# Softmax denominators of most blocks: from TensorE matmuls to a DMA transpose and GpSimd sums

## The chip, the cores and the metric

The kernel runs on one core of a Trainium2 chip, in one launch. The metric is the device time in microseconds of that core, lower is better. A profile is one execution recorded by the hardware profiler; its span runs from the first to the last instruction of the program.

## What is computed

Four batches of 12,544 tokens with 128 channels go through an induced attention block and then through a max-out feed-forward layer:

```
x: (4, 12544, 128)   inducing: (32, 128)   w1, w2: (128, 1024)   w_out: (1024, 128)
mab(q, kv):  a = softmax(q kv^T / sqrt(128));  return a @ kv
h   = mab(inducing, x)          # per batch: 32 rows
y   = mab(x, h)                 # per batch: 12544 rows, softmax over the 32 rows of h
out = max(y @ w1, y @ w2) @ w_out
```

The second softmax has 32 terms for each token. Its denominator is one number for each token: the sum of 32 exponentials. The kernel keeps the exponentials unnormalised through the whole feed-forward layer and divides each output row by its denominator at the very end.

## The kernel before

**Tiling.** A batch is 98 chunks of 128 tokens. Chunks are taken in blocks of at most sixteen: a block has four quarters, and a quarter has up to four chunks. There are 28 blocks. For each block `stage` writes one tile `e2` of 128 partitions by 512: partition 32 q + m holds the exponential of inducing row m for the tokens of quarter q, and column 128 t + j is token j of the quarter's chunk t. Block 0 and blocks later than it go through these steps:

- `phase` (matmuls on L990): small matmuls with 32 rows of weights, four quarters side by side, give (w2 - w1) applied to y for all 1024 hidden columns; ScalarE (L1006) or VectorE (L1009) turns each PSUM bank of 512 columns into a `relu` tile. In the same rows a matmul with `m1` (also L990) starts the output bank with the linear part.
- `final_one` (L809): 8 matmuls of 128 x 128 for each chunk add the relu part to the output bank; 3,136 in all. This is most of TensorE's work.
- `evict_group` (L836): VectorE multiplies the output bank of a group (mostly 4 chunks) by `rp`, the reciprocal of the denominators, into an `o` tile (5 buffers), and SyncE stores it (L861).
- `dens` is called by `final_one` when the first group of a block is about to start and the block has no `rp` yet. It serves the block, and the next one too if that is staged. For each chunk column t it runs one full matmul on L641 with 128 columns of `e2` as weights against `ones_q`, 128 x 4, and one VectorE reciprocal (L651) then writes `rp`.

**Next batch.** While batch b is worked on, batch b+1 is prepared: GpSimd issues seven loads (`load_x`, L165), SyncE issues 14 DMA transposes of `x` into `xT` (`transpose_x_dma`, L171), TensorE takes the scores (`pool_scores`, L308), SyncE transposes their exponentials `eu` into `eT` (`pool_turn`, L345) in six pieces, and TensorE sums with them (`pool_accum`, L364), two pieces v = u-1, u for each call.

**Order.** All five engines have a hand order (`manual_schedule`). The program is written out by a loop that keeps a small clock of its own (`ck`) for TensorE, ScalarE and VectorE and chooses the next piece from it; side jobs stand in a list `pending` and are issued when `ready` says so; a table `DEV` changes the choice at some steps. So the order is fixed when the program is built, and each engine and each DMA queue works through its own list in that order. SyncE's list holds the stores, the transposes of `x` and the transposes of `eu`; an entry that waits holds all behind it.

Of the kernel before, what the change touches and what calls it, by code (L numbers as in the profile page):

```python
# [9 lines left out]
F16 = mybir.dt.float16  # L10
F32 = mybir.dt.float32
AF = mybir.ActivationFunctionType
ALU = mybir.AluOpType
# [3 lines left out]
INF = 1e9  # L17
# [85 lines left out]
def kernel(  # L103
# [9 lines left out]
    nc = tc.nc  # L113
    B, N, C = x.shape
    M = inducing.shape[0]
# [10 lines left out]
    consts = ctx.enter_context(tc.tile_pool(name="consts", bufs=1))  # L126
    big = ctx.enter_context(tc.tile_pool(name="big", bufs=1))
    etp = ctx.enter_context(tc.tile_pool(name="etp", bufs=3))
    e2p = ctx.enter_context(tc.tile_pool(name="e2p", bufs=NE2))
    smp = ctx.enter_context(tc.tile_pool(name="smp", bufs=2))  # L130
    relup = ctx.enter_context(tc.tile_pool(name="relup", bufs=2))
    outp = ctx.enter_context(tc.tile_pool(name="outp", bufs=5))
# [41 lines left out]
        st[b]["T", j] = ck.pe  # L174

    identity16 = consts.tile([128, 128], F16, name="identity16")
    identity32 = consts.tile([128, 128], F32, name="identity32")
    ones32 = consts.tile([128, 128], F32, name="ones32")
    ones16 = consts.tile([128, 128], F16, name="ones16")
    warm = consts.tile([128, 512], F16, name="warm")  # L180
    ones_q = consts.tile([128, 4], F16, name="ones_q")

    ind_sb = consts.tile([M, C], F32, name="ind_sb")
    w2h = relup.tile([128, 4096], F16, name="w2h", tag="relu0")[:, 0:J]
    w1h = relup.tile([128, 4096], F16, name="w1h", tag="relu1")[:, 0:J]
    w21 = consts.tile([C, J], F16, name="w21")
# [2 lines left out]
    w1out = consts.tile([C, C], F16, name="w1out")  # L189
    inducingT = consts.tile([C, M], F16, name="inducingT")  # L190
    m1bd = consts.tile([128, 4, C], F16, name="m1bd")
    rep32 = consts.tile([128, 128], F32, name="rep32")
    repd = consts.tile([128, 128], F32, name="repd")
    diag = consts.tile([128, M], F32, name="diag")
    pace = consts.tile([128, 1], F32, name="pace")

    with tc.manual_schedule(engines={ET.PE, ET.DVE, ET.Activation, ET.Pool, ET.SP}):
# [14 lines left out]
        nc.gpsimd.dma_start(out=woutp, in_=moe_w_out.rearrange("(jb j) c -> j jb c", j=128))  # L212
        nc.vector.memset(warm, 0.0)
        nc.vector.memset(ones16, 1.0)
        nc.vector.memset(ones32, 1.0)
        nc.vector.memset(ones_q, 0.0)
        for q in range(4):
            nc.vector.memset(ones_q[32 * q : 32 * (q + 1), q : q + 1], 1.0)
# [129 lines left out]
        def pool_accum(b, u):  # L348

            bi, ps = bank([128, 512])  # L350
            ck.wait(ck.bank[bi], "p1")
            last = u == NU - 1
            if u == 1:
                st[b]["hacc"] = smp.tile([128, C + 1], F32, name=f"hacc_{b}", tag="hacc")
            acc = st[b]["hacc"]
            if last:
                nc.vector.reduce_sum(out=acc[:, C : C + 1], in_=st[b]["es"], axis=AX.X)
                ck.on_dve(st[b]["eu", u][1], 0.1)
            for v in (u - 1, u):
                eT = st[b]["eT", v][0]  # L360
                st[b]["sum", v] = True
                for j in range(4):
                    for g in range(4):
                        nc.tensor.matmul(  # L364
                            out=ps[32 * g : 32 * (g + 1), 0:128],
                            lhsT=eT[:, j, 32 * g : 32 * (g + 1)],
                            rhs=xn_of(b, U * v + 4 * g + j),
                            start=(j == 0 and v < u),
                            stop=(j == 3 and v == u and not (last and g < REST)),
                            tile_position=(0, 32 * g),  # L370
                            skip_group_check=True,
                        )
            if last:
                et = st[b]["et"][0]
                for g in range(4):
                    pairs = [(warm[:, 0:M], ones16[:, 0:1], 128, 1)]
                    if g < REST:
                        pairs = [
                            (et[:, g, :], xn_of(b, U * NU + g), 0, 128),
                            (et[:, g, :], ones16[:, 0:1], 128, 1),  # L380
                        ]
                    for lhsT, rhs, lo, n in pairs:
                        nc.tensor.matmul(
                            out=ps[32 * g : 32 * (g + 1), lo : lo + n],
                            lhsT=lhsT,
                            rhs=rhs,
                            start=False,
                            stop=True,
                            tile_position=(0, 32 * g),
                            skip_group_check=True,  # L390
                        )
            end = ck.run(0.58 if last else 0.49, "col")
            n = C + 1 if last else C
            if u == 1:
                nc.vector.tensor_copy(out=acc[:, 0:n], in_=ps[:, 0:n])
            else:
                nc.vector.tensor_add(out=acc[:, 0:n], in0=ps[:, 0:n], in1=acc[:, 0:n])  # L397
            ck.bank[bi] = ck.on_dve(end, 0.22)
            if last:
                st[b]["esrr"] = ck.bank[bi]  # L400
            if last and b + 1 < B:
                for i in range(7):
                    load_x(b + 1, i, acc[:, C : C + 1] if i == 0 else None)

# [115 lines left out]
        def weights_1b():  # L520
            for h in range(2):
                nc.gpsimd.tensor_sub(w21[:, 512 * h : 512 * (h + 1)], w_of[h][0], w_of[h][1])
# [44 lines left out]
        for b in range(B):  # L567
# [6 lines left out]
                blocks.append(Block(quarters, (0,) if not blocks else (0, 1, 2, 3) if shape == (4, 3, 2, 1) else ()))  # L574
            assert c0 == K

        def stage(blk):
            bi, ps = bank([128, 512])
            wd = blk.width
            some = [qu for qu in blk.quarters if qu]  # L580
            ck.wait(max(ck.bank[bi], st[some[0].b]["hT4r"]), "stage bank")
            for q in range(4):
                qu = blk.quarters[q] or some[0]
                hq = st[qu.b]["hT4"][:, 32 * q : 32 * (q + 1)]
                xT = xT_tiles[qu.b % 2]
                lo = qu.c0 if qu.c0 + wd <= K else K - wd
                pieces = [(0, qu.c0, min(wd, K - qu.c0))]
                if pieces[0][2] < wd:
                    pieces.append((pieces[0][2], lo, wd - pieces[0][2]))
                for t, c, n in pieces:  # L590
                    nc.tensor.matmul(  # L591
                        out=ps[32 * q : 32 * (q + 1), 128 * t : 128 * (t + n)],
                        lhsT=hq,
                        rhs=xT[:, c : c + n, :],
                        start=True,
                        stop=True,
                        tile_position=(0, 32 * q),
                        skip_group_check=True,
                    )
            end = ck.run(0.054 * wd, "col")  # L600
            uid[0] += 1
            blk.e2 = e2p.tile([128, 512], F16, name=f"e2_{uid[0]}", tag="e2")
            nc.scalar.activation(  # L603
                out=blk.e2[:, 0 : 128 * wd], in_=ps[:, 0 : 128 * wd], func=AF.Exp,
                scale=st[0]["rs"] if blk.b == 0 else scale,
            )
            blk.staged = ck.bank[bi] = ck.on_act(end, 0.05 + wd * 128 / 1200.0)
            blk.staged = max([blk.staged] + [st[qu.b].get("hwdr", 0.0) for qu in some])
        relu_of = {}

        def relu_slot(blk, q):
# [110 lines left out]
        groups = [g for _, _, g in sorted(groups, key=lambda e: e[:2])]  # L722
        for n, g in enumerate(groups):
            g.blk.last_group[g.q] = n
        state = {"g": 0, "mm": 0, "lin": 0, "done": 0, "issued": 0}
        ptr = [[0, 0] for _ in range(4)]
        chunks_done = [0]

# [203 lines left out]
        def phase(jobs):  # L932
            free = sorted(range(8), key=lambda j: ck.bank[j])
            got = []
            for j in jobs:
                while j[0] == "L" and "m1" not in st[j[2].blk.b]:
                    f, a = pending.pop(0)
                    f(*a)
            for (kind, q, a, u), bi in zip(jobs, free):
                _, ps = bank([128, 512], only=bi)  # L940
# [73 lines left out]
                state["issued"] += 1  # L1014

        jobs_at, due = {}, {}
        DONE0 = [0, 98, 196, 294]

        def at(n, f, *a):
            jobs_at.setdefault(n, []).append((f, a))  # L1020
            if f in (pool_scores, pool_accum):
                due[f, a] = n
# [21 lines left out]
                at(base + int(t_first + t_step * j), transpose_x_dma, b, j)  # L1044

        pending = []

        def ready(f, a):

            d = st[a[0]]  # L1050
            now = ck.pe
            if f is pool_scores and a[1] >= NEU and ("eT", a[1] - NEU) not in d:
                return False
            if f is pool_turn and a[1] >= NEU and ("sum", a[1] - NEU) not in d:
# [72 lines left out]
        phase(plan_phase(False))  # L1127
        pending.append((small_m1, (0,)))
        state["stage"] = 2
        weights_1b()  # L1130
        START = ck.pe
        step = -1
        while state["g"] < len(groups) or held:
# [24 lines left out]
            if tp < INF and lag() <= 128 + LIMIT and now:  # L1158
                if how != 3 and column_work(len(jobs) + 1, how == 4):
                    continue  # L1160
                phase(jobs)
            elif tf < INF:
                keep_busy(tf)
                ck.wait(tf, "relu")
                final_one()
            elif tp < INF:
                phase(jobs)
            elif pending:
                f, a = pending.pop(0)
                f(*a)  # L1170
            else:
                raise AssertionError(("stuck", state, ptr, chunks_done, jobs, pending[:3]))
        assert not pending and not jobs_at

# [28 lines left out]
```

## Time and profile before

| | |
|---|---|
| median of 3 runs | 327.38 us (327.37 to 327.85) |
| profiled execution, span | 325.6 us |
| outside the span: median less span | 1.7 us |
| TensorE busy | 319.8 us, 98% of the span |
| VectorE busy | 283.1 us, 87% |
| ScalarE busy | 281.7 us, 87% |
| GpSimd busy | 25.6 us, 8% |
| denominators: matmuls on L641, reciprocals on L651 | 102 and 15 |
| DMA | 53.65 MB, mean 165 GB/s |

The profile page has no time of its own for the profiled execution besides the span; what lies around the span is taken as the difference to the median of the runs. PE is TensorE, DVE VectorE, ACT ScalarE, POOL GpSimd, SP SyncE; PEld are the weight loads of TensorE, which overlap its matmuls, and SPq is SyncE's queue. Matmuls are pipelined, so a matmul's duration is longer than the distance from its start to the start of the next one; what a matmul costs the stream is that distance.

### The profile page before, as it was taken

The numbers are of one execution on the slowest core, as the hardware profiler recorded it, in microseconds if no ns is written. First come the engines' busy times: TensorE is split into PE (matmuls) and PEld (weight loads), VectorE is DVE, ScalarE is ACT, GpSimd is POOL, SyncE is SP. The second block draws the span as 40 slices with busy tenths as digits, with TensorE's granted clock in tenths as the row PEclk, the third lists the DMA queues.
The fourth block names the chain that finished last, engine by engine and source line by source line (L and its number), as shares of the span: only waits on it lengthen the run. The fifth ranks groups of instructions, "written<-read, shape, count | busy, mean of one in ns | idle before, by whom it ended". The sixth has DMA issues, their size and how long they took to land.

```text
span 325.6 us, 12570 instructions
## 1 busy us (share of the span) xinstructions
PE 319.8 (98%) x5404; PEld 243.0 (75%) x5404; DVE 283.1 (87%) x509; ACT 281.7 (87%) x560; POOL 25.6 (8%) x51
## 2 busy tenths in 40 slices
PE   7999999999999999999999999999999999999996
PEld 3876777777767777777777777777777777778785
DVE  3359989989989998998989999998989999999973
ACT  3679899999989899998888999989969999999961
POOL 7452030000040000000040000000000000000000
PEclk9999999999999999999999999999999999999999
DMA  8999999976279999993389999992312312222233
GB/s 204 208 206 214 286 246 212 172 207 134 97 150 245 225 248 209 201 203 86 116 162 243 214 234 232 190 192 86 115 66 101 113 68 98 90 108 99 85 115 112
DMA packets 70823, 53.65 MB, mean 165 GB/s; under 512 B 52176, under 2 KB 55408, under 8 KB 70768
## 3 DMA queue, kind: packets, MB, share of 16 engines
q1 hardware_dynamic: 64656, 38.63, 49.2%
q0 software_dynamic: 6112, 14.22, 22.3%
q8 instruction: 42, 0.69, 0.9%
q14 instruction: 13, 0.11, 0.1%
HBM read 28.33 MB, written 25.69 MB: 166 GB/s over the span
## 4 chain that ended last, share of the span: by engine, by line
PE 95%; DVE 1%; DMA 1%; ACT 0%; issue 0%; ACTq 0%; DVEq 0%
PE ps L809 61%; PE ps L990 22%; PE ps L591 2%; PE ps L232 2%; PE ps L308 2%; PE ps L364 1%; DMA xf<-in_x_dram 1%; PE ps L248 1%; DVE relu L1009 1%; PE ps L280 1%; PE ps L641 1%; PE ps L766 1%; PE ps L271 1%; PE ps L657 0%; PE ps L473 0%; PE ps L409 0%
## 5 line engine op out<-in xcount | busy, mean ns | idle before, releaser
L1006 ACT ACTIVATE relu<-ps 128x512 f16<-128x512 f32 x461 | 244.8, 602 | 26.6 <-PE ps L990 18.1
L1009 DVE TENSOR_SCALAR relu<-ps 128x512 f16<-128x512 f32 x323 | 206.8, 682 | 16.9 <-PE ps L990 15.3
L809 PE MATMUL ps<-woutp,relu 128*128 128x128 f16 x3136 | 217.3, 220 | 0.0
L809 PEld LDWEIGHTS <-relu 128*128 128x128 f16 x3136 | 176.7, 98 | 39.6 <-issue 29.1
L990 PE MATMUL ps<-e,hwd 32*128 32x512 f16 (+2 forms) x880 | 88.7, 360 | 0.0
L836 DVE TENSOR_TENSOR o<-ps,rp 128x512 f32<-128x512 f32 (+3 forms) x108 | 68.5, 634 | 5.5 <-PE ps L809 3.4
L990 PEld LDWEIGHTS <-hwd 32*128 32x128 f16 x880 | 24.9, 91 | 21.1 <-issue 1.0
L990 PE MATMUL ps<-m,e 32*128 32x128 f16 x381 | 38.8, 217 | 0.0
L990 PEld LDWEIGHTS <-e 32*128 32x128 f16 x381 | 21.3, 93 | 2.6
L165 POOL DMA_DIRECT2D xn<-in_x_dram x31 | 17.0, 557 | 8.2 <-DMA xn<-in_x_dram 4.3
L236 DVE COPY xT<-ps 128x512 f16<-128x512 f16 (+3 forms) x11 | 5.5, 504 | 7.8 <-PE ps L232 7.7
L319 ACT ACTIVATE eu<-ps 128x512 f16<-128x512 f32 x18 | 10.8, 615 | 0.0
L603 ACT ACTIVATE e<-ps 128x512 f16<-128x512 f32 (+2 forms) x21 | 10.5, 577 | 0.0
L164 POOL COPY pace<-hacc 128x1 f32<-128x1 f32 x2 | 0.4, 184 | 114.8 <-DVE hacc L397 114.8
L591 PE MATMUL ps<-xT,hT 128*32 128x512 f16 (+3 forms) x114 | 8.9, 362 | 0.0
L239 ACT COPY xT<-ps 128x768 f16<-128x768 f16 (+3 forms) x11 | 6.1, 556 | 2.7 <-PE ps L232 2.6
L232 PE MATMUL ps<-identity,xn 128*128 128x128 f16 x98 | 7.4, 219 | 0.4 <-DVE xn L661 0.3
L232 PEld LDWEIGHTS <-xn 128*128 128x128 f16 x98 | 5.6, 97 | 1.6 <-DVE xn L661 1.1
L257 ACT ACTIVATE et<-ps 128x448 f16<-128x448 f32 (+4 forms) x11 | 4.5, 413 | 2.6 <-PE ps L248 2.6
L308 PE MATMUL ps<-xT,inducingT 128*32 128x512 f16 x72 | 6.5, 385 | 0.0
L591 PEld LDWEIGHTS <-hT 128*32 128x32 f16 x114 | 3.3, 94 | 4.1 <-issue 3.0
L364 PE MATMUL ps<-xn,eT 128*32 128x128 f16 x288 | 5.5, 220 | 0.0
(96 smaller groups left out, 108.2 us busy)
## 6 DMA issues: line engine op xcount, KB each, us to landing
out_dram<-o SPq DMA_DIRECT2D x90, 256.0 KB, 2.4
xn<-in_x_dram POOLq DMA_DIRECT2D x24, 448.0 KB, 11.8
out_dram<-o SPq DMA_DIRECT2D x10, 128.0 KB, 3.0
xn<-in_moe_w_dram POOLq DMA_DIRECT2D x4, 256.0 KB, 14.1
xn<-in_x_dram POOLq DMA_DIRECT2D x4, 224.0 KB, 10.2
xT<-xn SPq DMA_TRANSPOSE x42, 4.3
xf<-in_x_dram SPq DMA_DIRECT2D x1, 512.0 KB, 3.9
xf<-in_x_dram SPq DMA_DIRECT2D x1, 384.0 KB, 4.3
```

The lines of the kernel that those rows point to most:

```text
L165: nc.gpsimd.dma_start(out=xn_at[b, i][:, 0:n, :], in_=xr[b, :, k0 : k0 + n, :])
L232: nc.tensor.transpose(ps[:, j, :], xn[:, g + j, :], identity16)
L308: nc.tensor.matmul(out=ps[32 * g : 32 * (g + 1), :], lhsT=inducingT, rhs=xT_tiles[b % 2][:, U * u + 4 * g : U * u + 4 * (g + 1), :], start ...
L319: nc.scalar.activation(out=eu, in_=ps, func=AF.Exp, scale=scale, accum_out=st[b]["es"][:, u : u + 1])
L364: nc.tensor.matmul(out=ps[32 * g : 32 * (g + 1), 0:128], lhsT=eT[:, j, 32 * g : 32 * (g + 1)], rhs=xn_of(b, U * v + 4 * g + j), start=(j = ...
L591: nc.tensor.matmul(out=ps[32 * q : 32 * (q + 1), 128 * t : 128 * (t + n)], lhsT=hq, rhs=xT[:, c : c + n, :], start=True, stop=True, tile_p ...
L603: nc.scalar.activation(out=blk.e2[:, 0 : 128 * wd], in_=ps[:, 0 : 128 * wd], func=AF.Exp, scale=st[0]["rs"] if blk.b == 0 else scale,)
L809: nc.tensor.matmul(out=g.ps[:, 128 * c : 128 * (c + 1)], lhsT=g.blk.relu[q][:, 128 * (jb * w4 + t) : 128 * (jb * w4 + t + 1)], rhs=woutp[: ...
L836: nc.vector.tensor_mul(osb[:, 0:n, :], g.ps[:, 0 : n * C].rearrange("p (s c) -> p s c", s=n), rp)
L990: nc.tensor.matmul(**seq[i])
L1006: nc.scalar.activation(out=dst, in_=src, func=AF.Relu)
L1009: nc.vector.tensor_scalar(out=dst, in0=src, scalar1=0.0, scalar2=None, op0=ALU.max)
```

## The change

For 20 of the 28 blocks the denominators no longer come from TensorE. When such a block is staged, a job `turn_e2` is put in `pending`. It issues on SyncE a DMA transpose of the `e2` tile into `ed` (token on the partition, then chunk, quarter and the 32 terms), and on GpSimd five additions that halve the 32 terms step by step (16, 8, 4, 2, 1) and one `pow` with exponent -1; the result `rd` takes the place of `rp`. `dens` is unchanged and serves the blocks that have no `rp` when their first group starts.

`ready` lets a `turn_e2` go only if at least 20 chunks of earlier blocks are still to be finished, the block is staged, the last turn was at least 9 us before and the last loads of the next batch at least 22 us before (all on the builder's clock); turns start after 18 chunks. The subtraction of the weights on GpSimd (`weights_1b`) is issued at that point too, in the same place of GpSimd's list. To make room in SBUF, the constants that are needed at the start alone (`identity32`, `rep32`, `ind_sb`, `diag`) share the first buffer of `relu3`, `ones16` shrinks and `ones32` goes.

The core of the diff:

```diff
+    edp = ctx.enter_context(tc.tile_pool(name="edp", bufs=2))
...
-    identity32 = consts.tile([128, 128], F32, name="identity32")
-    ones32 = consts.tile([128, 128], F32, name="ones32")
-    ones16 = consts.tile([128, 128], F16, name="ones16")
+    head = relup.tile([128, 4096], F16, name="head", tag="relu3").bitcast(F32)
+    identity32 = head[:, 0:128]
+    rep32 = head[:, 128:256]
+    ind_sb = head[0:M, 256:384]
+    diag = head[:, 384:416]
+    ones16 = consts.tile([128, 2], F16, name="ones16")
...
+    minus1 = consts.tile([128, 16], F32, name="minus1")
...
             if last and b + 1 < B:
+                state["loads"] = ck.pe
                 for i in range(7):
                     load_x(b + 1, i, acc[:, C : C + 1] if i == 0 else None)
...
+            if state.get("turns"):
+                pending.append((turn_e2, (blk,)))
+
+        def turn_e2(blk):
+
+            if blk.rp is not None:
+                return
+            state["turned"] = ck.pe
+            wd = blk.width
+            uid[0] += 1
+            ed = edp.tile([128, 4, 128], F16, name=f"ed_{uid[0]}", tag="ed")
+            nc.sync.dma_start_transpose(
+                ed[:, 0:wd, :], blk.e2[:, 0 : 128 * wd].rearrange("p (j t) -> p j t", j=wd)
+            )
+            den = edp.tile([128, 16], F32, name=f"den_{uid[0]}", tag="den")
+            half = edp.tile([128, 16, 16], F32, name=f"half_{uid[0]}", tag="half", bufs=1)
+            cur = ed[:, 0:wd, :].rearrange("p j (q m) -> p (j q) m", q=4)
+            n = M // 2
+            while n >= 1:
+                dst = half[:, 0 : 4 * wd, 0:n] if n > 1 else den[:, 0 : 4 * wd, None]
+                nc.gpsimd.tensor_tensor(out=dst, in0=cur[:, :, 0:n], in1=cur[:, :, n : 2 * n], op=ALU.add)
+                cur = half[:, 0 : 4 * wd, :]
+                n //= 2
+            rp = edp.tile([128, 4, 4], F32, name=f"rd_{uid[0]}", tag="rd", bufs=7)
+            nc.gpsimd.tensor_tensor(
+                out=rp[:, 0:wd, :].rearrange("p t q -> p (t q)"),
+                in0=den[:, 0 : 4 * wd],
+                in1=minus1[:, 0 : 4 * wd],
+                op=ALU.pow,
+            )
+            blk.rp = rp[:, 0:wd, :]
+            blk.turned = ck.pe
...
+        def turns_on():
+            weights_1b()
+            state["turns"] = True
...
+        at(18, turns_on)
...
+            if f is turn_e2:
+                blk = a[0]
+                if blk.rp is not None:
+                    return True
+                ahead = sum(len(g.chunks) for g in groups[state["g"] :] if g.blk.index < blk.index)
+                return ahead >= 20 and blk.staged <= now and state["turned"] + 9.0 <= now and state["loads"] + 22.0 <= now
...
-        weights_1b()
```

## The prediction

> **What bounds the kernel now.** I read the page's busy shares and its chain first.
>
> ```profile
> PE 319.8 (98%) x5404; PEld 243.0 (75%) x5404; DVE 283.1 (87%) x509; ACT 281.7 (87%) x560; POOL 25.6 (8%) x51
> ```
>
> ```profile
> PE 95%; DVE 1%; DMA 1%; ACT 0%; issue 0%; ACTq 0%; DVEq 0%
> ```
>
> TensorE is busy for nearly all of the span and is 95% of the chain that ended last. A busy PE need not be a full PE, so the waits come next.
>
> ```profile
> ACT relu L1006 <- PE ps L990: 18.1, 45, 1.9
> DVE relu L1009 <- PE ps L990: 15.3, 35, 1.5
> ...
> PEld L809 <- DVE relu L1009: 0.3, 1, 0.3
> ```
>
> ScalarE and VectorE wait for TensorE (18.1 and 15.3 us); TensorE waits for a relu once, 0.3 us. TensorE's own stream is the bound, so what it no longer issues is gained in full, and any wait put in its way is lost in full. Then one place where denominators are made, from the timeline (start, length, instructions), and the two lines as such:
>
> ```profile
> 104.72 0.45 PE L809 MATMUL ps<-woutp,relu 128*128 128x128 f16 x5
> 105.01 0.34 PE L641 MATMUL ps<-ones_q,e 128*128 128x4 f16 x8
> 105.21 0.78 PE L809 MATMUL ps<-woutp,relu 128*128 128x128 f16 x11
> ```
>
> ```profile
> L641 PE MATMUL ps<-ones_q,e x102: 163/165/168, 25.9 to 316.7; 128*128 128x4 f16 x102
> ```
>
> Eight matmuls hold the stream from 105.01 to 105.21: 25 ns each, not the 165 ns that one lasts, since they overlap.
>
> **TensorE: what goes.** The order in which the changed kernel's instructions stand has 32 matmuls for denominators, at 5 places, instead of 102 at 15. The runs of matmuls between switches of kind (222 of the L990 kind, 26 of scores and sums) are as many as before. So 70 x 25 ns = 1.8 us goes, all on the path.
>
> A rule of the Trainium skill would make it more: "TensorE: Matmul & The Clock Gate", section "LDWEIGHTS (loading the stationary operand)", takes a weight load of 128 columns as 128/1.2 = 107 ns, so that 70 would be an estimated 7.5 us; here the load lies under other work, and the 25 ns of the timeline decide.
>
> **VectorE.** Ten reciprocals go: six of 348 ns, two of 297, two of 274, together 3.2 us. VectorE waits 15.3 us for TensorE as it is, so this brings nothing. One relu moves from VectorE to ScalarE (0.60 us against 0.68), hidden by the 18.1 us that ScalarE waits.
>
> **SyncE: what comes.** Twenty transposes, sixteen of them 4 x 128 columns like those of `eu` on L345:
>
> ```profile
> 64.01 2.57 SPq L861 DMA_DIRECT2D out_dram<-o  x3
> 66.67 2.64 SPq L345 DMA_TRANSPOSE eT<-eu  x2
> 69.41 0.53 SPq L861 DMA_DIRECT2D out_dram<-o  x1
> 70.03 2.54 SPq L345 DMA_TRANSPOSE eT<-eu  x2
> 72.66 2.10 SPq L861 DMA_DIRECT2D out_dram<-o  x2
> ```
>
> Two take 2.63 us until the next issue (70.03 to 72.66), 1.3 us each. The queue goes from one issue to the next without a pause from 50 to 76 us, so a transpose put in there moves all behind it by 1.3 us. The guard keeps turns off the loads, where stores have least room (at 93 to 106 and 165 to 176 us a store lands 0.7 to 2.5 us before its `o` buffer is needed; at the turns it is 5 us and more), but not off the transposes of `x` and `eu`. In the built order one turn stands behind the eighth transpose of `x` (52.8 us), one behind the fourteenth (64.0), one behind the second of `eu` (69.4), one behind the fifth. So the third and fourth of `eu` come 3 x 1.3 = 3.9 us later. The view of L345 in 71.2 to 72.6 us has these two, and TensorE's timeline their reader:
>
> ```profile
> DMA to landing us min/median/max: 2.4/3.2/4.0
> ```
>
> ```profile
> 77.15 1.08 PE L364 MATMUL ps<-xn,eT 128*32 128x128 f16 x64
> ```
>
> The fourth is issued at 71.3 and lands 4.0 us later, 75.3; the last 16 of the 64 matmuls read it, at 77.8. In the changed kernel they come at 77.6 (8 matmuls fewer before) and the issue at 75.2. With a landing of 2.4 us there is no wait (77.6), with 4.0 it is 1.6 us, with the middle of the two, 3.2, it is 0.8 us. I take 0.8: the same piece behind the same neighbours took 4.0, its twin 2.4.
>
> The next narrowest places: the scores at 61.1 read a transpose issued at 54.8 that landed at 59.5; 1.3 us later is 60.8, against 60.9: nothing, 0.5 us if it is unlucky. The sums at 138.4 read an `eu` transpose that landed at 135.1, behind two turns: 137.7, against 138.4 less 0.6 plus the 0.8 lost before: nothing. The others have over 1.5 us left by the same count.
>
> **GpSimd and the wait on it.** The first eviction of a turned block (L836) now waits for `rd`; behind it in VectorE's list stand the relus of the following phases, and TensorE waits for those. Chain: issue, landing (2.3 to 4.2 us for `eu`, median 2.8), five additions and a power. The nearest rows:
>
> ```profile
> L522 POOL TENSOR_TENSOR w<-xn,xn 128x512 f16<-128x512 f32 x2 | 2.5, 1270 | 10.3 <-DMA xn<-in_moe_w_dram 10.3
> L164 POOL COPY pace<-hacc 128x1 f32<-128x1 f32 x2 | 0.4, 184 | 114.8 <-DVE hacc L397 114.8
> ```
>
> Six instructions are at least 6 x 0.18 = 1.1 us and, if each cost as much as 512 columns, 7.6 us. The additions have 256 columns down to 16: estimated 0.65, 0.4, 0.3, 0.2, 0.2; no row has a power on GpSimd, I take 0.6 for it: 2.4 us, nearer the copy's end since five of six are short. With 2.8 the chain is 5.2 us. Room: the first turn from 52.8 to the eviction at 63.9, 11.1 us; the second from 65.3 to 75.6, 10.3; the fifth 119.0 to 131.7, 12.7; the others 14.8 (the fourth, 80.2 to 95.0) and more. Covered; even 7.6 + 2.8 is 10.4.
>
> A rule speaks against it: "GPSIMD Engine Reference", section "Instruction dispatch", puts the first call of a freshly loaded kernel at about 6 us of code loading; that would make the first chain an estimated 11.2 us and cost 0.1 us once. L522's first subtraction (1.27 us, the second 1.27) shows nothing of the kind, and no row here has the power.
>
> **At nothing.** `weights_1b` keeps its place in GpSimd's list (41 us), and its reader, L473, starts at 92.7. The start constants in `relu3` are last read at 22.2 us (L449), before the first relus; were they read later, the first relu of that buffer would wait. The memsets of the start change size only.
>
> **Sum.** Against the profiled execution: 325.6 - 1.8 + 0.8 = 324.6 us of span; with the 1.7 us around it, 326.3. The span and these 1.7 us make the median of the runs, 327.4, so the sum holds for it as well.
>
> **Rivals.**
> *A turn costs the queue more than its issue* (slower). If the next transpose only gets going when the turn has landed (2.3 us at least), the pushes are 6.9 instead of 3.9 us at the same sums, and the wait there grows from 0.8 to 3.8 us: 327.4 - 1.8 + 3.8 = 329.4. It turns the result slower from a wait of 2.5 us, that is a push of 1.9 us a turn. For it: the 16 DMA engines are busy for 0.96 of the stretch from 46 to 82 us, and one transpose held the queue 5.67 us at 107.1. Against it: transposes issued 1.3 us apart each landed in 2.3 to 4.2.
> *GpSimd's chain is longer than its room.* A power that takes 6 us more makes the chain 11.2 us: 0.1 us at the first, 0.9 at the second turn, 327.3. At 14 us of chain it would be 2.9 + 3.7 + 1.3 = 7.9 us. For it: no row; against it: five of the six are plain additions and all but three turns have over 14 us.
> *The matmuls filled time in which TensorE would wait anyway*: 327.4. The waits (0.3 us for a relu) speak against it.
>
> **Chances.** The forecast has 0.72: 0.60 with a wait up to 1.1 us, 0.12 with more, up to 1.6 (no change). Slow turns 0.13 (0.10 slower, 0.03 no change), GpSimd 0.08 (0.04 and 0.04), no gain 0.07. A measurement of this kernel tells about 0.2%, 0.65 us: faster is below 326.73, slower above 328.03. Faster 0.60, same 0.26, slower 0.14. The range goes from 325.3 (no wait anywhere, 325.6, and 0.3 us of the small gaps that ten reciprocals fewer may close) to 328.2, with 0.12 left out above and some 0.05 below.
>
> **What would show it.** L641 x32, L651 x5 and about 1.0 us of the stream at the first; a wait of TensorE for a DMA (`eT`) near 78 us, at most 1.6 us; L836 never waiting for GpSimd; six GpSimd instructions in 2 to 3 us. Wrong it would be if evictions wait for `rd`, if stores hold VectorE by their `o` buffer, or if L364 or L308 wait for longer than 2.5 us.

## The result, and the profile after

The changed kernel takes 329.05 us, the median of 22 runs (327.44 to 332.16); the kernel before took 327.58 us in the runs beside it. The ratio is 1.0044, with an interval of 1.0024 to 1.0065: slower, where the forecast was faster. The profiled execution has a span of 327.5 us against 325.6.

The engines' busy times and the chain that ended last, from the changed kernel's page:

```profile
PE 319.5 (98%) x5334; PEld 241.4 (74%) x5334; DVE 280.1 (86%) x498; ACT 281.8 (86%) x561; POOL 113.2 (35%) x171
```

```profile
PE 91%; DMA 4%; DVE 3%; ACT 1%; issue 1%; SPq 0%; DVEq 0%; ACTq 0%
```

Busy times hardly move, except GpSimd's. The chain says more: TensorE's share falls from 95% to 91%, DMA's rises from 1% to 4% and VectorE's from 1% to 3% (2% with the gain alone and with GpSimd alone, below, which wait for no transfer). The view of the waits names the transfers (engine and line waiting, releaser: total us, times, longest us):

```profile
PEld L366 <- DMA eT<-eu: 2.7, 2, 2.1
...
PEld L332 <- DMA xT<-xn: 0.6, 1, 0.6
```

L366 are the sums (L364 before), L332 the last scores of a batch. Neither line was in the waits of before. The timeline shows the worst place; first the changed kernel's transpose of `eu` on SyncE's queue and the matmuls that read it, then the same transpose before:

```profile
138.30 1.23 SPq L347 DMA_TRANSPOSE eT<-eu  x1
...
138.48 0.40 PE L366 MATMUL ps<-xn,eT 128*32 128x128 f16 x16
...
140.82 0.41 PE L366 MATMUL ps<-xn,eT 128*32 128x128 f16 x16 [1.95 <-DMA eT<-eu]
```

```profile
132.66 1.22 SPq L345 DMA_TRANSPOSE eT<-eu  x1
```

TensorE arrives as early as before, at 138.5 us, but the transpose is issued 5.6 us later, lands at 140.8, and 2.1 us of the stream are lost. Two smaller waits, 0.56 us at 77.9 and 0.55 us at 224.3, are of the same kind. From start to start over the whole trace: the denominators' matmuls give back 1.78 us (2.76 to 0.98), the groups of sums, with their two waits, cost 2.91 us more, the wait at 224 costs 0.55, the start 0.3, small shifts 0.1, and the end is 0.25 us shorter. Together that is about the 1.86 us between the spans.

Why the transpose comes 5.6 us later is in SyncE's queue (start, length, instructions), first in the changed kernel, then before:

```profile
115.98 2.58 SPq L172 DMA_TRANSPOSE xT<-xn  x1
...
120.67 1.21 SPq L625 DMA_TRANSPOSE ed<-e  x1
...
124.54 2.76 SPq L172 DMA_TRANSPOSE xT<-xn  x1
127.40 0.53 SPq L898 DMA_DIRECT2D out_dram<-o  x1
127.98 1.28 SPq L172 DMA_TRANSPOSE xT<-xn  x1
129.36 1.21 SPq L625 DMA_TRANSPOSE ed<-e  x1
...
131.29 3.60 SPq L172 DMA_TRANSPOSE xT<-xn  x2
```

```profile
115.44 1.26 SPq L171 DMA_TRANSPOSE xT<-xn  x1
...
121.61 1.25 SPq L171 DMA_TRANSPOSE xT<-xn  x1
...
123.54 1.99 SPq L171 DMA_TRANSPOSE xT<-xn  x1
...
126.26 2.62 SPq L171 DMA_TRANSPOSE xT<-xn  x2
...
130.91 1.67 SPq L171 DMA_TRANSPOSE xT<-xn  x1
```

A turn (L625) takes 1.21 us and 0.1 us to the next issue, as forecast, and the queue goes on without waiting for it to land. But some transposes of `x` last 2.3 to 2.8 us instead of 1.28. The push of 5.64 us is made of 2.6 for two turns, 0.5 from before 115 us, and a net 2.5 for such long issues (1.3, 1.5 and 1.0 more at 116.0, 124.5 and 132.6, less 1.3 for the ones that the kernel before had in this stretch). At each of the three a 16 KB packet of the instruction-fetch queue starts within 0.7 us of the issue's start. Of the 179 issues after 45 us, 19 last over 0.5 us longer than usual for their kind, and 17 of these have such a packet in flight, though only 38 of the 179 have one, since there are only 36 packets, 0.9 to 2.0 us each, in that time; the kernel before has 13 of 16. No experiment took the fetches away, so this is a coincidence in time, not a cause that is shown. The long issues also differ between executions: two traces of one kernel (the later sums, below) have 63.7 and 68.9 us for the 42 issues of `xT`.

### The profile page after: what moved, and what is told of

It reads as the page before. It is cut to its first block, busy times and chain, and to the rows that moved or that the text cites. A ratio compares the mean times of both kernels' runs of the same rounds, so it can differ in the third digit from the quotient of the medians.

```text
span 327.5 us, 12613 instructions
## 1 busy us (share of the span) xinstructions
PE 319.5 (98%) x5334; PEld 241.4 (74%) x5334; DVE 280.1 (86%) x498; ACT 281.8 (86%) x561; POOL 113.2 (35%) x171
## 4 chain that ended last, share of the span: by engine, by line
PE 91%; DMA 4%; DVE 3%; ACT 1%; issue 1%; SPq 0%; DVEq 0%; ACTq 0%
PE ps L846 58%; PE ps L1027 21%; PE ps L596 2%; PE ps L234 2%; DMA eT<-eu 2%; PE ps L310 1%; DVE relu L1046 1%; DMA xf<-in_x_dram 1%; DMA xT<-xn 1%; PE ps L366 1%; PE ps L250 1%; PE ps L282 1%; DVE o L873 1%; PE ps L694 1%; ACT relu L1043 1%
## 5 line engine op out<-in xcount | busy, mean ns | idle before, releaser
L634 POOL TENSOR_TENSOR half<-ed 128x256 f32<-128x256 f16 (+2 forms) x20 | 12.1, 605 | 150.2 <-DMA ed<-e 150.2
L638 POOL TENSOR_TENSOR rd<-den,minus 128x16 f32<-128x16 f32 (+2 forms) x20 | 52.0, 2598 | 1.6
L873 DVE TENSOR_TENSOR o<-ps,rd 128x512 f32<-128x512 f32 (+1 forms) x76 | 47.2, 624 | 4.9 <-PE ps L846 2.7
L873 DVE TENSOR_TENSOR o<-ps,rp 128x512 f32<-128x512 f32 (+3 forms) x32 | 21.0, 656 | 0.1
L634 POOL TENSOR_TENSOR half<-half 128x32 f32<-128x32 f32 (+4 forms) x60 | 19.2, 321 | 4.7
L366 PE MATMUL ps<-xn,eT 128*32 128x128 f16 x288 | 5.9, 221 | 2.3 <-DMA eT<-eu 2.3
```

What stands on the lines that cost most here:

```text
L634: nc.gpsimd.tensor_tensor(out=dst, in0=cur[:, :, 0:n], in1=cur[:, :, n : 2 * n], op=ALU.add)
L638: nc.gpsimd.tensor_tensor(out=rp[:, 0:wd, :].rearrange("p t q -> p (t q)"), in0=den[:, 0 : 4 * wd], in1=minus1[:, 0 : 4 * wd], op=ALU.pow,)
L873: nc.vector.tensor_mul(osb[:, 0:n, :], g.ps[:, 0 : n * C].rearrange("p (s c) -> p s c", s=n), rp)
```

## The experiments

All ratios are to the kernel before on the same chip. The first four take the change apart. Where GpSimd's sums are left out, the turned blocks are scaled by 1; where only the transposes are, by sums of other numbers. The cost-alone kernel computes both kinds of denominators and uses TensorE's.

**The gain alone: no transposes and no GpSimd sums.** The transpose, the additions and the power are removed.

```diff
-            nc.sync.dma_start_transpose(ed[...], blk.e2[...])
-            ... additions, power
-            blk.rp = rp[:, 0:wd, :]
+            blk.rp = one16[:, 0:wd, :]
```

> The changed kernel without its DMA transposes and without the GpSimd sums: the 20 blocks divide by a tile of ones, so their rows are not normalised; TensorE's list is that of the changed kernel (32 denominator matmuls). Queue theory (the saving on TensorE is real, and the loss is TensorE waiting for transposes that SyncE's queue issues late): 70 x 25 ns = 1.8 us below the kernel before, ratio 0.9945, no wait of L366 for a DMA. Cover theory (the 70 matmuls filled time that TensorE would have waited anyway): ratio 1.000. GpSimd theory (the sums on GpSimd slow VectorE or hold the evictions): like the queue theory here, 0.9945.

326.51 us, 0.9973 (0.9964 to 0.9983). The 70 matmuls go (0.98 us left for 32) and nothing waits, but only 0.9 us of 1.8 arrive in the median, 1.3 in the profiled span: in the last next batch the builder now chooses another order, and the matmuls around the side jobs take about 0.5 us more.

**The cost alone: all turns and sums, but all 102 matmuls too.**

```diff
-            if blk.rp is not None:
+            if hasattr(blk, "turned"):
...
-            blk.rp = rp[:, 0:wd, :]
             blk.turned = ck.pe
```

> The kernel before with all of the additions and none of the savings: 20 DMA transposes and 120 GpSimd instructions are issued, their result is not used, and all 102 denominator matmuls and 15 reciprocals stay. Queue theory: the waits of the changed kernel at 78, 139 and 224 us (0.56 + 2.12 + 0.55 = 3.2 us) come on top of the kernel before, a little less since TensorE arrives up to 0.6 us later at each: ratio 1.006 to 1.010. GpSimd theory, with evictions held by the sums: ratio 1.000, as nothing waits for the sums; with VectorE slowed by GpSimd: above 1.004. Cover theory: 1.004.

332.97 us, 1.0157 (1.0125 to 1.0189), well above the expectation, and not at the expected places: its profile has no wait at 78 or 139 us but waits of 1.1, 1.1 and 2.0 us that end at 148, 227 and 229 us, and right after the last two the granted clock is 0.5 for 3.41 us (below). With other places of the waits, and the clock on top, cost alone and gain alone don't sum to the change.

**The transposes alone, without GpSimd, and GpSimd alone, without the transposes** (the sums read `e2` as it lies).

```diff
# transposes alone
-            ... additions, power
-            blk.rp = rp[:, 0:wd, :]
+            blk.rp = one16[:, 0:wd, :]
# GpSimd alone
-            nc.sync.dma_start_transpose(ed[...], blk.e2[...])
-            cur = ed[:, 0:wd, :].rearrange("p j (q m) -> p (j q) m", q=4)
+            cur = blk.e2[:, 0 : 128 * wd].rearrange("p (g m) -> p g m", m=M)
```

> The changed kernel with its 20 DMA transposes but without the GpSimd sums; the 20 blocks divide by a tile of ones, so their rows are not normalised. Queue theory: as the changed kernel, ratio to the kernel before 1.003 to 1.006, with waits of L366 for a DMA of 2 to 3 us. GpSimd theory: 0.9945.

> The changed kernel without the DMA transposes; GpSimd's 120 instructions run on the untransposed tile (they add neighbouring tokens, so the 20 blocks are divided by wrong numbers), and the evictions wait for their result as in the changed kernel. Queue theory: ratio 0.9945, as in the run without both. GpSimd theory: as the changed kernel, 1.003 to 1.006.

Transposes alone: 329.37 us, 1.0058 (1.0034 to 1.0082), with waits of 0.84, 1.89 and 0.76 us at the changed kernel's three places and two more of 0.38 and 0.33 us at 149 and 154 us:

```profile
PEld L368 <- DMA eT<-eu: 3.3, 4, 1.9
...
PEld L334 <- DMA xT<-xn: 1.1, 2, 0.8
```

GpSimd alone: 325.99 us, 0.9957 (0.9942 to 0.9971), and no wait for a transfer. The loss is the transposes'; GpSimd is covered.

**One chunk for each turn instead of four.** The same queue order as with the transposes alone, with a quarter of their work (no GpSimd sums, scaled by 1 again).

```diff
-                ed[:, 0:wd, :], blk.e2[:, 0 : 128 * wd].rearrange("p (j t) -> p j t", j=wd)
+                ed[:, 0:1, :], blk.e2[:, 0:128].rearrange("p (j t) -> p j t", j=1)
```

> The twenty transposes of turned blocks stay where they are in SyncE's list, but each takes one chunk of 128 columns instead of four; no GpSimd sums, and the turned blocks are scaled by 1. Everything else stands in the order of the transposes-alone kernel (1.0058, waits of 0.84 us at 77 and 1.89 us at 138 us). Theory one, a turn costs the queue its own issue of 1.3 us and that does not depend on the columns: the pushes and waits stay, ratio 1.003 to 1.007. Theory two, the cost is the work that a four-chunk transpose puts on the 16 DMA engines (0.84 us of all sixteen), which backs up into the queue when an instruction fetch comes: a quarter of that is left, the issue of the sums' transpose at 138 us comes less than 2 us later than in the kernel before, no wait over 0.3 us there, ratio 0.996 to 0.999.

328.21 us, 1.0017 (1.0000 to 1.0035), between the two expectations. The profiled execution is the slowest of the twelve (326.90 to 330.37 us) and shows what the first expects: the sums' transpose near 138 us is pushed by 5.42 us, and the wait stays. It doesn't tell whether the wait is there in the faster ones. First this kernel's queue, then its waits:

```profile
120.42 1.19 SPq L627 DMA_TRANSPOSE ed<-e  x1
...
124.28 2.42 SPq L172 DMA_TRANSPOSE xT<-xn  x1
```

```profile
PEld L368 <- DMA eT<-eu: 3.0, 2, 2.3
```

One chunk takes 1.19 us of issue where four took 1.21. The long issues stay as well, so they don't need all of the turns' bytes. The lower ratio (1.0017 against 1.0058 with the transposes alone) suggests that part of the loss, in some executions, does go with the work on the DMA engines.

**Two turns fewer before the wait at 139 us.**

```diff
+                if ("T", 4) in st[2] and ("eT", 1) not in st[2]:
+                    return False
                 return ahead >= 20 and ...
```

> The changed kernel without the two turns between the fifth transpose of x for batch 2 and its second transpose of eu (18 turns, 40 denominator matmuls on TensorE). If the wait of 2.1 us at 138.7 us comes from the push of SyncE's queue by these turns, it goes (below 0.3 us), the eu transpose that these sums read is issued no more than 1 us later than before, and the time falls by 1.5 to 2.2 us against the changed kernel less 0.2 us for the eight matmuls: ratio to the kernel before 0.997 to 1.000. If the wait came from GpSimd or from the changed order on TensorE, it stays and the ratio is 1.003 to 1.006.

330.41 us, 1.0081 (1.0054 to 1.0108): a miss, not faster than with the two turns. The mechanism at 139 us was right: the push there is 2.1 us instead of 5.6 and the wait is gone. The one at 78 us stays (0.9 us), and a long one comes back further on (waits, then the timeline; the bracket is the wait):

```profile
PEld L332 <- DMA xT<-xn: 2.4, 1, 2.4
```

```profile
224.59 0.22 PE L332 MATMUL ps<-inducingT,xT 128*128 128x32 f16 x2 [2.21 <-DMA xT<-xn]
```

In the next batch the queue is still pushed by 6.9 us (8.2 in the changed kernel). TensorE, no longer held up at 139 us, reaches the last scores at 222.2 us instead of 224.3 and finds the transpose of `x` missing. In the changed kernel the first wait had paid for most of the second. Soon after the wait the clock is 0.5 for 3.41 us too.

**Turns only where nothing is behind them, and the opposite.** A turn may go only while no batch has transposes of `x` or `eu` under way (11 turns, 68 matmuls left), or only while one has (14 turns, 54 left). The two don't add up to 20, since a turn that has to wait for a quiet time can come at a place where the changed kernel has none.

```diff
+                quiet = all(("T", 0) not in s or ("eT", NU - 1) in s for s in st[1:])
-                return ahead >= 20 and ...
+                return quiet and ahead >= 20 and ...        # the other: not quiet
```

> A turn is issued only while no batch has transposes of x or eu under way: 11 turns instead of 20, 68 denominator matmuls instead of 32, so 34 x 25 ns = 0.87 us go from TensorE's stream. If the turns cost only through the transposes of x and eu queued behind them, no wait for eT or xT over 0.3 us is left and the ratio is 0.996 to 0.999. If a turn costs something wherever it stands (its stores, GpSimd, the clock), the ratio is 1.000 or more.

> The opposite of the kernel with 11 quiet turns: a turn is issued only while some batch has transposes of x or eu under way, at the same places as in the changed kernel. 14 turns, 54 denominator matmuls left, so 48 x 25 ns = 1.2 us go from TensorE; the places of scores and sums in TensorE's order are those of the changed kernel. If a turn costs only by what is queued behind it, all of the changed kernel's loss is here: waits for eT near 78 us (0.3 to 1 us) and 139 us (1.9 to 2.3 us), and the ratio is that of the changed kernel plus 0.55 us for 22 matmuls: 1.004 to 1.008, where the 11 quiet turns had 0.9994. If the cost is the same for each turn wherever it stands, the ratio is near 1.001.

Quiet: 327.35 us, 0.9994 (0.9981 to 1.0008), no wait for a transfer. The others: 330.27 us, 1.0092 (1.0056 to 1.0128), with the view of the waits

```profile
PEld L366 <- DMA eT<-eu: 3.8, 3, 2.5
...
PEld L332 <- DMA xT<-xn: 0.7, 1, 0.7
```

So the loss sits with the 14 turns that have transposes behind them. Two misses remain: the quiet kernel was to save 0.87 us and shows 0.2, and the other lost more than the expected 1.004 to 1.008.

**The quiet kernel in fewer groups.** It had 31 groups of 32-column matmuls (27 before); one guard, 10.5 instead of 9.5 for one sum, makes them 26.

```diff
-                return d.get(("eT", a[1]), (0, INF))[1] + 9.5 <= now and ...
+                return d.get(("eT", a[1]), (0, INF))[1] + (10.5 if a == (1, 3) else 9.5) <= now and ...
```

> The kernel with 11 quiet turns (0.9994) with one number more: the builder's guard for the fourth sum of the first next batch is 10.5 instead of 9.5. On TensorE this leaves the 68 denominator matmuls and 222 phases as they are, but the pieces of 32-column matmuls (scores, sums, stages) stand in 26 groups instead of 31; the kernel before has 27. In the profile of the 31-group kernel a step from the phases to such a group lasted 0.17 us longer than the median of its kind. If these changes of kind ate the 0.87 us that the quiet turns save, five groups fewer give back 0.8 to 1.7 us: ratio 0.995 to 0.998, faster than both kernels, and no wait for eT or xT over 0.3 us. If the shortfall has another cause, the ratio stays at 0.999 to 1.001.

327.49 us, 1.0006 (0.9993 to 1.0019). The time doesn't fall with the changes of kind, but its profile (328.50 us, among the slower third) also has a new wait of 1.3 us for `eT` at 224 us, so they are not ruled out. What eats 0.4 to 0.7 us in kernels whose order was re-chosen stays open.

**The waiting sums later, all turns kept.**

```diff
-                return d.get(("T", 13), INF) + 6.0 <= now
+                return d.get(("T", 13), INF) + 7.0 <= now
-                return d.get(("eT", a[1]), (0, INF))[1] + 9.5 <= now and ...
+                return d.get(("eT", a[1]), (0, INF))[1] + {(1, 3): 11.0, (2, 1): 14.0}.get(a, 9.5) <= now and ...
```

> All 20 turns stay; only the sums that waited are taken later by the builder's guard: two of them by 1.5 and 4.5 us, the last scores by 1 us. TensorE then finds other matmuls to do while the transposes land. If the loss is only the waits at 78, 139 and 224 us, these fall below 0.3 us each and the kernel comes to the gain-alone kernel (ratio 0.9973) or a little above: 0.996 to 0.999, faster than both kernels. If the pushed queue moves the waits elsewhere (loads, stores, o buffers), the ratio stays at 1.002 or more.

327.40 us, 1.0008 (0.9984 to 1.0032), from 326.07 to 330.48. The profiled execution, 326.39 us, has no wait. A second profile of it, 327.61 us, had one of 0.5 us at 79.5:

> The kernel with the later sums a second time, for one more profile: its twelve runs lay in two groups, 326.1 to 326.9 us (no wait in the one that was profiled) and 327.9 to 330.5 us. If the pushed queue still reaches its readers in some executions, a profile of the second group shows a wait of TensorE for eT or xT of 1 to 3 us, behind issues of SyncE that last over 2 us; if the second group has another cause, there is no such wait.

It fell between the two groups of times, so the upper group's cause stays open. The slowest of the twelve runs before, 330.48 us, has a mean clock of 0.995, as the traces with a long wait have.

**The turns from ScalarE's queue.**

```diff
-            nc.sync.dma_start_transpose(
+            nc.scalar.dma_start_transpose(
```

> The changed kernel with one word changed: the twenty transposes of turned blocks are issued from ScalarE's queue instead of SyncE's. Orders on TensorE, VectorE, GpSimd and of all other entries are the same. If the loss is the issue time of 1.2 us each in SyncE's queue, then the transposes of x and eu keep the issue times of the kernel before (the eu transpose read at 138 us within 1 us of 132.7), the waits at 78, 139 and 224 us fall below 0.3 us each, and TensorE gains up to 1.8 us; ScalarE carries 20 x 1.2 = 24 us more beside 18 to 20 us that it spends waiting for TensorE, so what of it shows as a wait of TensorE for a relu or a bank is the open cost, 0 to 3 us: ratio 0.995 to 1.003. If the loss came from the transfers themselves on the DMA engines, whichever queue issues them, the waits for eT stay at 1.5 us or more.

411.06 us, 1.2547 (1.2523 to 1.2571), a miss for both theories. The waits, and TensorE at the first turn:

```profile
ACT relu L1043 <- DMA out_dram<-o: 28.1, 5, 8.0
```

```profile
54.04 0.61 PE L1027 MATMUL ps<-e,hwd 32*128 32x512 f16 x2 [6.50 <-ACT relu L1043]
```

In the built program a transpose on one queue waits until transfers issued before it on the other have landed, and the other's next transpose waits for it. ScalarE stands up to 8.0 us with its relus behind it, and TensorE waits for those. SyncE's transposes of `x` in turn wait for the turns:

```profile
SPq L172 <- DMA ed<-e: 30.7, 8, 4.6
```

The granted clock is also 0.50 for 78.5 us of this trace, by estimate up to 39 us of what was lost. The Trainium skill has a rule that would explain such waits ("DMA: Bandwidth & Descriptors", section "Silent corruption: two transposing streams in flight at once"): transposes of two queues must not be in flight together, so the later stream has to wait for the earlier one's completion. The waits above agree with it (30.7 us at eight transposes of `x`). On ScalarE's queue, then, the 1.3 us of a turn can't be had for nothing.

**Fewer issues with the same bytes.** The tiles of `x` are transposed by one DMA of 14 chunks instead of two of 7, in the changed kernel and, as a control, in the kernel before.

```diff
-        nc.sync.dma_start_transpose(
-            xT_tiles[b % 2][:, k0 + m * h : k0 + m * (h + 1), :], xn_at[b, i][:, m * h : m * (h + 1), :]
-        )
+        if h == 0:
+            nc.sync.dma_start_transpose(xT_tiles[b % 2][:, k0 : k0 + n, :], xn_at[b, i][:, 0:n, :])
```

> The changed kernel with its 20 turns, but each tile of x (14 chunks) is transposed by one DMA instead of two of 7 chunks; every order on TensorE, VectorE, ScalarE and GpSimd stays. This takes 21 issues of 1.2 to 1.3 us out of SyncE's list, as many as the turns put in. If the loss is the number of issues ahead of the transposes of eu and x in that list (one-chunk turns cost as much as four-chunk turns), the eu transpose read at 139 us is issued before 133 us again, no wait for eT or xT over 0.3 us is left, and the kernel comes to the gain-alone kernel: ratio 0.996 to 0.998, faster than both. If a transpose of 14 chunks takes twice the issue of one of 7, or the bytes on the DMA engines set the queue's pace, the pushes and the wait of 2 us at 139 us stay: 1.003 to 1.006.

> The same change to the kernel before: its x tiles transposed by 21 DMAs of 14 chunks instead of 42 of 7. TensorE waits there for no transpose, so a shorter list in SyncE's queue has nothing to give: 0.999 to 1.001. If the kernel gets faster by more than 0.2%, SyncE's queue cost it time that its profile doesn't show as a wait; if it gets slower, the 14-chunk transposes do harm of their own (later landing of a tile's first half), and the other run must be read with that.

With all 20 turns: 325.83 us, 0.9953 (0.9939 to 0.9966), from 325.66 to 325.96, faster than both kernels. Control: 326.81 us, 0.9988 (0.9979 to 0.9996), slightly better than expected, from a source that its profile doesn't show. Between these two the change gains 0.98 us. The chain of the first is that of a kernel without waits, and the sums at 138 us run through:

```profile
PE 95%; DVE 2%; DMA 1%; ACT 1%; issue 0%; ACTq 0%; DVEq 0%
```

```profile
134.42 1.74 SPq L346 DMA_TRANSPOSE eT<-eu  x1
...
137.46 0.62 PE L365 MATMUL ps<-xn,eT 128*32 128x128 f16 x32
```

The size was off: the transpose is issued at 134.4, not before 133, since a 14-chunk transpose isn't as short as one of 7 (line of the transposes of `x`, this kernel and the changed one; minimum, median, maximum in ns):

```profile
L173 SPq DMA_TRANSPOSE xT<-xn x21: 1447/2223/6510, 34.6 to 211.7; - x21
```

```profile
L172 SPq DMA_TRANSPOSE xT<-xn x42: 1226/1299/5671, 35.2 to 221.4; - x42
```

All issues of `xT` together take 57.7 us instead of 72.9, against 26.3 us for the turns. That is enough: the last transpose of `x` of each batch is issued 1.1 us earlier, 0.3 later and 1.4 earlier than in the kernel before, where the changed kernel was 1.8, 7.9 and 8.2 us late.

## Why the prediction was wrong, step by step

- **TensorE, 1.8 us:** right in the stream (2.76 to 0.98 us), too high in the result. Gain alone, GpSimd alone and the pair with 14-chunk transposes show 0.9, 1.4 and 1.0 us. As many runs of matmuls as before isn't the same order.
- **VectorE and the relu moved, nothing:** right; its relus last 682 ns in both kernels and no eviction waits for GpSimd.
- **SyncE, the step that failed.** That a turn "moves all behind it by 1.3 us" held for the turn itself. What failed is to count only turns. At the fourth `eT` the push was 4.7 us where 3.9 were forecast; there the wait (0.56 us, forecast 0.8) came out near the forecast by luck, because the transpose landed in 2.4 us where the forecast counted with 3.2. At the sums at 138 us, "137.7, against 138.4 less 0.6 plus the 0.8 lost before: nothing", the push was 5.6 where 2.6 were forecast, and the wait 2.1 us. Issues of 2.3 to 2.8 us among the entries behind shift with the queue, and a margin of under 1 us was no margin. The forecast had seen a range of landings (2.4 to 4.0 us) but no range of issues, although its own trace had one of 5.67 us and several of 2.
- **"The others have over 1.5 us left":** failed at 224 us (push 8.2 us, wait 0.55 us), and two fewer turns show 2.4 us there once the wait at 139 us is gone.
- **GpSimd:** covered, as forecast, with a wrong term. The power was put at 0.6 us and takes 2.9 for a full block; the six instructions of the first turn take 5.2 us, not 2.4.

```profile
L638 POOL TENSOR_TENSOR rd<-den,minus x20: 1017/2910/2937, 58.4 to 302.4; 128x16 f32<-128x16 f32 x16, 128x8 f32<-128x8 f32 x2, 128x4 f32<-128x4 f32 x2
```

  The first power took 2.94 us, the median 2.91, so the weighed rule of 6 us for a first call is not seen here.
- **The rival "a turn costs the queue more than its issue"**, at 329.4 us and with a chance of 0.13, came true in its result (329.05) and its test (a wait over 2.5 us in all), not in its mechanism: the next issue starts 0.1 us after a turn ends, and what costs more are other entries.

## What to carry to other kernels

When something is put into an in-order queue, sum the queue as it will be, entry by entry with the spread of their issue times, down to each reader's deadline, and treat a margin smaller than that spread as a wait. A wait that is removed can turn up at the next reader if the queue behind it stays late, so pushes have to be followed through all stages, not to the first deadline. If a full queue is the limit, making its other entries fewer and larger may be worth more than moving the new ones.

## What the runs showed of the hardware

- **A transpose's issue depends little on its size at first:** in the median 1.18 us for one chunk of 128 columns, 1.21 for four and 1.30 for seven, but 2.22 for fourteen (1.45 at least).
- **A wait of about 2 us on TensorE can cost the clock as well.** In every trace the granted clock changes only at whole multiples of 3.41 us from the start of its record, so the time falls into windows of that length. Two windows in the trace with one-chunk turns, then two with the turns that have transposes behind them, around the wait near 139 us (window, its length, busy time of PE, PEld, DVE, ACT, POOL, the granted clock, DMA share, GB/s):

```profile
138.43:141.84 3.41, 1.32 (x37) 0.73 (x30) 1.15 (x3) 1.74 (x6) 0.00 (x0) 1.00 0.82 189
141.84:145.25 3.41, 3.41 (x37) 2.93 (x34) 2.30 (x4) 2.29 (x6) 0.00 (x0) 0.50 0.45 104
```

```profile
137.41:140.82 3.41, 1.69 (x38) 1.07 (x36) 2.48 (x5) 2.83 (x7) 0.00 (x0) 1.00 0.79 185
140.82:144.23 3.41, 2.86 (x57) 2.05 (x58) 1.73 (x4) 1.96 (x5) 0.00 (x0) 1.00 1.19 184
```

  The first wait, 2.26 us, lies almost wholly in one window, TensorE is busy for 1.32 us of it, and the next window runs at half the clock. The second wait, 2.45 us, is longer but lies across a border; its first window is busy for 1.69 us, and the clock stays at 1.00. All 16 traces together agree: of the windows at the full clock, the 27 with at most 1.67 us of matmuls are followed by half the clock, the other 1,476 are not. So the border is near half of a window (the ends of matmuls are modelled, so it isn't known more sharply), and how a wait lies in the windows counts, not its length alone. The way back takes a window that is busy for 3.40 us or more (15 of 15; after 11 windows with up to 3.24 us the clock stayed at half). At half the clock 3.41 us cost an estimated 1.7 us more. Three of the changed kernel's 22 runs have a mean clock of 0.995, which is one such window: 330.84 to 332.16 us, against 327.44 to 330.99 us for the others. The Trainium skill ("TensorE: Matmul & The Clock Gate", "Part 1: The HAM clock gate") has windows of about 3.4 us that run freely; the length agrees. Its condition for the fall, at least one idle window, doesn't agree: the windows here were busy for up to 1.67 us.
- **Kernels with such waits spread more.** With turns among the transposes the runs lie 3.6 us apart (transposes alone) and 4.2 us (only the 14 turns); with none, or with 14-chunk transposes, 1.0, 1.2 and 0.3 us (gain alone, GpSimd alone, the fastest kernel, of which there are five runs). The kernel before, without waits, had one run at 331.72 us beside 21 from 327.14 to 328.36, so a slow run alone does not tell of a wait.
